# Later weights held back by a one-column copy, unit 1's scale inside unit 0's scan, stacking issued by two queues

## The chip, the cores and the metric

The kernel runs on one core of one Trainium2 chip. The metric is the device time of one execution in microseconds. A core has five engines that run beside each other, each through its own instructions in their given order: PE (TensorE, matmuls), DVE (VectorE), ACT (ScalarE), POOL (GpSimd) and SP (SyncE, which here only issues DMAs). They wait for each other through semaphores.

## What is computed

The reference runs a linear attention with a complex decay, token by token, and then a gated feed-forward layer. Batch B = 4, heads H = 8, sequence S = 768, head dimension D = 48; the layer is 384 to 1536 to 384.

```python
scale = np.minimum(mag, 0.999) / (mag + 1e-06)      # mag = |a|
a_re_n, a_im_n = (a_re * scale, a_im * scale)
for t in range(S):
    new_re = ar * S_re - ai * S_im                   # ar, ai: a at t, per head and row
    new_im = ar * S_im + ai * S_re
    S_re, S_im = (new_re + k_t v_t^T, new_im)
    y[:, :, t] = q_t @ S_re
out = ((x @ w_a) * (x @ w_b)) @ w_out                # x: y of all heads side by side
```

## The kernel before

**Units.** The sequence is cut into chunks of 128 tokens. A unit is one chunk of two of the batches, so there are NU = 12 units: units 0 to 5 are the six chunks of batches 0 and 1, units 6 to 11 those of batches 2 and 3. For each unit four things are done in turn:

1. `scale(u)` computes the factor that limits |a|, as a tile `sc` of 128 x 768: one wide square on ACT (L177), four logarithms and exponentials on ACT, and five operations on DVE (L178, L185, L188, L190, L192). In unit 0 it goes by two halves.
2. `prep(u)` multiplies a by `sc` (L210) and scans the products of the decay over the tokens: inside blocks of eight tokens (`pr` and `z`, L226 and L232, seven steps), then over the blocks through a chain of small operations `pb` and `b_t` (L261 and L267, eight pairs), then back over all tokens (L288, L293). From that it makes the scaled queries and keys in the tile `qk` (L308, L323). L277 writes the norm of the unit's decay, about the middle of `prep`. After its first lines it runs the scale of the next unit beside its own steps (the generator `sg`), but in unit 0 it does not: unit 1's scale is run at the head of `prep(1)` instead (L202 to L204). From here on, the moment when the last L308 of a unit has ended is called the moment its keys are there.
3. `stack(u)` moves `qk` by DMA into `stk`, with the real and imaginary rows of each head stacked on the partitions: ten transfers for the eight heads, two for heads 2 and 5 (L345, issued by SP).
4. `attn(u)` is the attention in 18 pieces: scores on PE (L378) times a mask on DVE (`am`, L381), transposes (L389), outputs (L418), copies of the output as a high part `xh` (L422) and the rest `xl` (L426, L429), and the running state (L437, L444).

**The feed-forward layer.** It takes fp32 operands as a high and a low part. For each unit, and for each of NF = 12 slices f of the hidden layer, `gemm1` does 18 matmuls (L481), then `h_t` and `hl` on DVE (L490, L492) and two copies on ACT (L489, L491), and `gemm2` 6 matmuls (L499), two slices later (LAG).

**The weights.** They arrive once, in 36 parts (12 slices by three matrices, 384 KB each; L124), as 64-bit words. Each part must be converted before its first use: three operations on DVE (L133, L135, L137) into one of three buffers `o_sb`, a cast of the high part on ACT (L141), a pair of matmuls on PE that leaves the low part (L146, L147), and a cast of it on ACT (L148). `split_weights` is a generator that converts one slice at each `next(ws)`.

**What sets the order.** A scheduler puts each engine's instructions into a fixed row before the kernel runs, by the order in which the code issues them, by priorities and by what it expects to be ready; the engine then takes its row strictly in order. The code issues the loads of all weights, scale 0, `prep(0)`, `stack(0)`, six slices of conversions, and then `attn(0)`, between whose pieces `prep(1)` runs on by 800 ns a piece (P1_A). Then come the slices of unit 0, with the other six conversions and the rest of `prep(1)`, 3000 ns a slice (P1_F); `stack(1)` and `attn(1)` follow inside them. The later units go the same way one unit ahead, without conversions.

The lines of issue that the change touches:

```python
    for f in range(3, NF):
        load_weights(f)
...
    drain(scale(0, a_tiles[0], z_first))
    drain(prep(0))
    stack(0)
    load_qk(1)
    p1 = prep(1)
    for _ in range(CONV_FIRST):
        next(ws)
    x_cur = new_x()
    for _ in attn(0, *x_cur):
        drain(p1, P1_A)
```

Of the kernel before, what the change touches and what calls it, by code (L numbers as in the profile page):

```python
# [8 lines left out]
F32 = mybir.dt.float32  # L9
# [13 lines left out]
NU = NBP * NCH  # L23
# [11 lines left out]
EPS = 1e-6  # L35
A2_MAX = 2.0 ** 60
ST = 8
P1_A = 800
P1_F = 3000
TOK = 2 * C  # L40
RUN = 2 * TOK + 2
NF = DF // 128
# [7 lines left out]
CONV_FIRST = 6  # L50
# [16 lines left out]
def tile_kernel(ctx: ExitStack, tc: tile.TileContext, a_d, qk_d, v_d, w_d, qn_d, kn_d, vn_d, an_d, out_d):  # L67
    nc = tc.nc
# [47 lines left out]
    raws = {}  # L116
# [1 line left out]
    def r(ap):  # L118
        return ap.bitcast(F32R)

    def load_weights(f):
        for m, (c0, n) in enumerate(WPART):
            raws[f, m] = wpool.tile([128, n, 2], U32, name=f"w{m}{f}")
            sync.dma_start(out=raws[f, m].rearrange("p c s -> p (c s)"),  # L124
                           in_=w_d[f, :, c0:c0 + n].bitcast(U32))

# [27 lines left out]
    def load_a(u):  # L154
        t = apool.tile([128, 2, W], F32, name="a_t")
        for hs in halves if u == 0 else (slice(0, W),):
            sync.dma_start(out=t[:, :, hs], in_=a_d[u, :, :, hs])
        return t

    a_tiles = {}  # L160
# [38 lines left out]
    def prep(u):  # L199
        c = u % NCH  # L200
        a_t = a_tiles.pop(u)
        if u == 1:  # L202
            yield from scale(u, a_t, a_first)
            a_tiles[u + 1] = load_a(u + 1)  # L204
        sc = sc_tiles.pop(u)
        z = zpool.tile([128, 3, W], F32, name="z") if u else z_first
        zz = z[:]
# [3 lines left out]
                              in1=sc.rearrange("p (b i e) -> p b i e", e=2, i=SUB // 2), op=ALU.mult)  # L211
        act.activation(out=z[:, 0], in_=z[:, 2], func=AF.Copy, scale=-1.0)  # L212
        yield 1700
        sg = scale(u + 1, a_tiles[u + 1], a_t) if 0 < u < NU - 1 else iter(())


        zb = z.rearrange("p s (j b e) -> p s j b e", j=SUB // 2, e=2)
# [116 lines left out]
    def load_qk(u):  # L334
        sync.dma_start(out=qk[:, :, 1, 0:2 * TOK], in_=qk_d[u])

    def stack(u):
        n = RUN if rescaled(u % NCH) else 2 * TOK
        for h in range(H):
            r0 = h * D  # L340
            while r0 < (h + 1) * D:
                j, p = divmod(r0, 128)
                m = min((h + 1) * D - r0, 128 - p)
                d0 = 2 * (r0 - h * D)
                sync.dma_start(out=stk[d0:d0 + 2 * m, h, 0:n], in_=qk[p:p + m, j, :, 0:n])  # L345
                r0 += m


# [249 lines left out]
    a_first = a_tiles[0] = load_a(0)  # L598
    load_weights(0)
    load_qk(0)  # L600
    load_weights(1)
    load_v(0)
    load_weights(2)
    a_tiles[1] = load_a(1)
    for f in range(3, NF):
        load_weights(f)

    def drain(gen, ns=None):
        if gen is None:
            return  # L610
        left = ns
        for cost in gen:
            if left is not None:
                left -= cost or 0
                if left <= 0:
                    return

    ws = split_weights()
    drain(scale(0, a_tiles[0], z_first))
    drain(prep(0))  # L620
    stack(0)
    load_qk(1)
    p1 = prep(1)
    for _ in range(CONV_FIRST):
        next(ws)
    x_cur = new_x()
    for _ in attn(0, *x_cur):
        drain(p1, P1_A)
    pend = []

    def second():
# [10 lines left out]
    for w in range(NU):  # L642
# [17 lines left out]

        for f in range(NF):
            if w == 0:
                next(ws, None)
                drain(p1, P1_F)
                if f == P1_AT:
                    drain(p1)
                    stack(1)
                    load_qk(2)
                    pgen = prep(2)
            pend.append((w, f, *gemm1(f, *x_cur), os_))  # L670
            slot()
            if len(pend) > LAG:
                second()
            slot()
            if f == STACK_AT[min(w, 4)]:
                drain(at)
                if w + 2 < NU:
                    drain(pgen)
                    stack(w + 2)
                if w + 3 < NU:  # L680
                    load_qk(w + 3)
                    pgen = prep(w + 3)
            if w > 0:
                drain(pgen, 2400)
# [70 lines left out]
```

## Time and profile before

| | |
|---|---|
| runs of the kernel | 700.78, 701.29, 702.23 us (median 701.29) |
| the profiled execution | 701.13 us, of it 699.4 from its first to its last instruction (the span) |
| granted clock of PE, mean | 0.984 |
| busy over the span | PE 656.8 us, DVE 541.8, ACT 320.2, POOL 5.6 |
| PE's first matmul of the feed-forward layer | 76.33 us |
| DMA read from and written to memory | 39.32 MB and 4.72 MB |

All times in the trace are microseconds from the start of the span. The page shows the span in 40 equal slices of 17.5 us; a digit is the busy share in tenths, and PEclk is the clock that PE was granted, in tenths of full speed:

```profile
PE   3547999999999999999999999999999999999996
DVE  6999899998889989899898989989899353232221
ACT  6357755735546255462554646356434222222221
PEclk9976999999999999999999999999999999999999
DMA  8963301513215033061431601520500500400000
```

PE is full from the fifth slice on. DVE is full from the second slice until the 29th, where the last unit's scan ends, and has little to do behind it. The weights and the first inputs come in during the first three slices. A busy PE is not PE at its peak, as matmuls overlap; what counts here is where it stands idle.

In the rows of the trace, a row that covers several instructions has a count (x2), and brackets hold an engine's idle time ahead of it and what ended that. The printed duration of a DVE operation reaches some 0.1 us into the next one, so what an operation takes from DVE is read from one start to the next.

### The profile page before, as it was taken

The numbers are of one execution on the slowest core, as the hardware profiler recorded it, in microseconds if no ns is written. First come the engines' busy times: TensorE is split into PE (matmuls) and PEld (weight loads), VectorE is DVE, ScalarE is ACT, GpSimd is POOL, SyncE is SP. The second block draws the span as 40 slices with busy tenths as digits, with TensorE's granted clock in tenths as the row PEclk, the third lists the DMA queues.
The fourth block names the chain that finished last, engine by engine and source line by source line (L and its number), as shares of the span: only waits on it lengthen the run. The fifth ranks groups of instructions, "written<-read, shape, count | busy, mean of one in ns | idle before, by whom it ended". The sixth has DMA issues, their size and how long they took to land.

```text
span 699.4 us, 14330 instructions
## 1 busy us (share of the span) xinstructions
PE 656.8 (94%) x5862; PEld 612.5 (88%) x5862; DVE 541.8 (77%) x1239; ACT 320.2 (46%) x642; POOL 5.6 (1%) x11
## 2 busy tenths in 40 slices
PE   3547999999999999999999999999999999999996
PEld 1214889899899999999999999999998999999996
DVE  6999899998889989899898989989899353232221
ACT  6357755735546255462554646356434222222221
POOL 3000000000000000000000000000000000000000
PEclk9976999999999999999999999999999999999999
DMA  8963301513215033061431601520500500400000
GB/s 316 402 258 100 112 1 46 147 44 110 87 38 182 17 120 101 16 189 46 120 100 45 168 24 46 152 82 5 163 24 13 154 24 17 106 23 2 23 1 28
DMA packets 30232, 63.94 MB, mean 91 GB/s; under 512 B 3664, under 2 KB 7248, under 8 KB 30160
## 3 DMA queue, kind: packets, MB, share of 16 engines
q1 hardware_dynamic: 26704, 58.23, 26.4%
q10 hardware_dynamic: 3456, 4.72, 1.8%
q8 instruction: 48, 0.79, 0.5%
q14 instruction: 24, 0.20, 0.1%
HBM read 39.32 MB, written 4.72 MB: 63 GB/s over the span
## 4 chain that ended last, share of the span: by engine, by line
PE 50%; DVE 38%; ACT 5%; DMA 3%; issue 2%; SPq 1%; DVEq 0%; ACTq 0%
PE ab L481 23%; PE o L499 12%; PE xp L418 4%; DVE a_t L288 4%; PE pm L378 4%; DVE qk L308 3%; DVE pr L226 3%; DVE hl L492 3%; DVE h_t L490 2%; PE pm L437 2%; DVE z L293 2%; DVE pb L261 2%; DVE z L232 2%; DMA stk<-qk 2%; PE pm L146 2%
## 5 line engine op out<-in xcount | busy, mean ns | idle before, releaser
L481 PE MATMUL ab<-xh,w 128*128 128x256 f32 x1728 | 339.3, 285 | 0.0
L481 PEld LDWEIGHTS ab<-xh,w 128*128 128x128 f32 x1728 | 276.9, 189 | 2.0 <-issue 1.4
L481 PE MATMUL ab<-xl,w 128*128 128x256 f32 x864 | 244.8, 283 | 0.0
L481 PEld LDWEIGHTS ab<-xl,w 128*128 128x128 f32 x864 | 163.0, 189 | 0.4
L499 PE MATMUL o<-w,hh 128*128 128x384 f32 x576 | 152.9, 345 | 0.0
L490 DVE TENSOR_TENSOR h_t<-ab,h_t 128x256 f32<-128x256 f32 x144 | 60.4, 419 | 80.0 <-ACT h_t L489 79.6
L489 ACT COPY h_t<-ab 128x256 f32<-128x256 f32 x144 | 53.3, 370 | 150.1 <-PE ab L481 149.1
L499 PEld LDWEIGHTS o<-w,hh 128*128 128x128 f32 x576 | 97.0, 188 | 3.5 <-issue 2.8
L491 ACT CAST hh<-h_t 128x256 fp32r<-128x256 f32 x144 | 58.0, 403 | 90.2 <-DVE h_t L490 89.6
L499 PE MATMUL o<-w,hl 128*128 128x384 f32 x288 | 97.4, 338 | 0.0
L492 DVE TENSOR_TENSOR hl<-h_t,hh 128x256 fp32r<-128x256 f32 x144 | 60.5, 420 | 20.6 <-ACT hh L491 20.5
L146 PE MATMUL ab<-o_sb,ident 128*128 128x384 f32 x42 | 28.7, 784 | 29.1 <-DVE o_sb L137 29.1
L378 PE MATMUL pm<-stk 128*128 128x128 f32 x384 | 53.6, 279 | 2.3 <-DMA stk<-qk 2.3
L499 PEld LDWEIGHTS o<-w,hl 128*128 128x128 f32 x288 | 54.1, 188 | 0.2 <-issue 0.2
L378 PEld LDWEIGHTS pm<-stk 128*128 128x128 f32 x384 | 48.7, 192 | 6.1 <-issue 3.9
L226 DVE TENSOR_TENSOR pr<-z 128x384 f32<-128x384 f32 (+1 forms) x91 | 47.2, 525 | 4.2 <-ACT z L212 2.1
L288 DVE TENSOR_TENSOR a_t<-z,b_t 128x768 f32<-128x768 f32 x48 | 44.3, 952 | 0.1
L146 PEld LDWEIGHTS ab<-o_sb,ident 128*128 128x128 f32 x42 | 9.7, 274 | 39.2 <-DVE o_sb L137 29.5
L418 PE MATMUL xp<-am,v_t 128*32 128x128 f32 x768 | 41.4, 277 | 2.3 <-DVE am L381 2.0
L308 DVE TENSOR_TENSOR qk<-qk,z 128x1536 f32<-128x1536 f32 (+1 forms) x26 | 42.4, 1629 | 0.1
L381 DVE TENSOR_TENSOR am<-pm,mask 128x512 f32<-128x512 f32 x48 | 32.8, 685 | 6.1 <-PE pm L378 6.1
L437 PE MATMUL pm<-v_t,kt 128*96 128x96 f32 x320 | 34.6, 250 | 0.1
(105 smaller groups left out, 766.4 us busy)
## 6 DMA issues: line engine op xcount, KB each, us to landing
w<-in_dram SPq DMA_DIRECT2D x36, 384.0 KB, 8.1
qk<-in_dram SPq DMA_DIRECT2D x12, 768.0 KB, 4.9
stk<-qk SPq DMA_DIRECT2D x48, 192.0 KB, 3.3
a_t<-in_dram SPq DMA_DIRECT2D x11, 768.0 KB, 4.4
v_t<-in_dram SPq DMA_DIRECT2D x24, 256.0 KB, 2.7
stk<-qk SPq DMA_DIRECT2D x24, 192.8 KB, 3.1
out_dram<-o_sb ACTq DMA_DIRECT2D x24, 192.0 KB, 1.9
stk<-qk SPq DMA_DIRECT2D x16, 128.0 KB, 3.2
```

The costliest lines, as they stand in the source:

```text
L146: pe.matmul(out=lp[:, 0:n], lhsT=ident, rhs=t, start=True, stop=False)
L226: vec.tensor_tensor(out=pr[:, :, :, o:o + n], in0=view(zz, W + at_(i) + 2 * o, [[W, 2], [-W, 2], [2, n]]), in1=tok(slice(1, 3), i - 1, o, ...
L288: vec.tensor_tensor(out=pz[:, s].rearrange("p (j b e) -> p j b e", j=SUB // 2, e=2), in0=zb[:, 1 + s], in1=view(bb, (1 + k - s) * NB, [[0, ...
L308: vec.tensor_tensor(out=qk4[:, :, k, x0:x1], in0=qk4[:, :, 1, x0:x1], in1=z[:, k].rearrange("p (j t) -> p j t", j=NJ).unsqueeze(2).broadca ...
L378: pe.matmul(out=sp[:, h4], lhsT=stk[:, h, ks], rhs=stk[:, h, qs], start=True, stop=True)
L418: pe.matmul(out=xp[qd * 32:(qd + 1) * 32, ti], lhsT=l, rhs=rr, start=st, stop=sp_, tile_position=(0, qd * 32), skip_group_check=True)
L481: pe.matmul(out=ab[:, m * TOK:(m + 1) * TOK], lhsT=r(w_ab(f, part, m * NJ + i)), rhs=r(xt[:, i, :]), start=n == 0, stop=n == 8)
L489: act.copy(out=h_t, in_=ab[:, 0:TOK])
L490: vec.tensor_tensor(out=h_t, in0=ab[:, TOK:2 * TOK], in1=h_t, op=ALU.mult)
L491: act.copy(out=r(hh), in_=h_t)
L492: vec.tensor_tensor(out=r(hl), in0=h_t, in1=hh, op=ALU.subtract)
L499: pe.matmul(out=os_[tt][:, 0:DM], lhsT=r(ht[:, ts]), rhs=r(w_t[f, 2][:, part, :]), start=(f == 0 and n == 0), stop=(f == NF - 1 and n == 2))
```

## The change

Four things are changed.

- **Weights held.** The loads of slices 0 to 2 stay at the start. Ahead of each part's load of slices 3 to 5, POOL now copies one column of unit 0's norm (written by L277 before, L276 after) into the part's buffer, and ahead of those of slices 6 to 11 one element a partition of unit 0's `qk`, where the keys' product L323 (L322 after) writes. The load overwrites the copy, so it must wait for it, and with it for that point of unit 0's scan. That makes 9 and 18 copies. SP issues the 18 behind its part of `stack(0)`.
- **Unit 1's scale** runs beside the steps of `prep(0)`; its input is loaded before the weights of slice 1, and unit 2's input right ahead of `stack(0)`'s transfers on SP.
- **Order of issue.** Three slices of conversions instead of six stand ahead of `attn(0)`, three more between its pieces, and `prep(1)` runs on only in the slices of unit 0, ahead of each slice's conversion.
- **Stacking of unit 0.** Odd heads are issued by ACT, even heads by SP. The other units' stay on SP.

```diff
+    def load_weights(f, after=None):
         for m, (c0, n) in enumerate(WPART):
             raws[f, m] = wpool.tile([128, n, 2], U32, name=f"w{m}{f}")
+            if after is not None:
+                nc.gpsimd.tensor_copy(out=raws[f, m].bitcast(F32)[:, 0, 0:1], in_=after)
             sync.dma_start(out=raws[f, m].rearrange("p c s -> p (c s)"),
...
-        if u == 1:
-            yield from scale(u, a_t, a_first)
-            a_tiles[u + 1] = load_a(u + 1)
...
-        sg = scale(u + 1, a_tiles[u + 1], a_t) if 0 < u < NU - 1 else iter(())
+        sg = scale(u + 1, a_tiles[u + 1], a_t) if u < NU - 1 else iter(())
...
-                sync.dma_start(out=stk[d0:d0 + 2 * m, h, 0:n], in_=qk[p:p + m, j, :, 0:n])
+                (act if u == 0 and h % 2 else sync).dma_start(out=stk[d0:d0 + 2 * m, h, 0:n], in_=qk[p:p + m, j, :, 0:n])
...
     load_qk(0)
+    a_tiles[1] = load_a(1)
     load_weights(1)
     load_v(0)
     load_weights(2)
-    a_tiles[1] = load_a(1)
-    for f in range(3, NF):
-        load_weights(f)
...
     drain(prep(0))
+    for f in range(3, CONV_FIRST):
+        load_weights(f, norms[:, 0, 0:1])
     stack(0)
+    for f in range(CONV_FIRST, NF):
+        load_weights(f, qk[:, 0, 1, TOK:TOK + 1])
     load_qk(1)
+    a_tiles[2] = load_a(2)
     p1 = prep(1)
-    for _ in range(CONV_FIRST):
+    for _ in range(3):
         next(ws)
     x_cur = new_x()
-    for _ in attn(0, *x_cur):
-        drain(p1, P1_A)
+    for n, _ in enumerate(attn(0, *x_cur)):
+        if n % 6 == 3:
+            next(ws)
...
             if w == 0:
+                drain(p1, P1_F)
                 next(ws, None)
-                drain(p1, P1_F)
```

How the rows of the engines move is shown at three places. Lines of the changed kernel are one or two off: L135, L137 and L139 are its conversion, L148 and L149 PE's pair, L344 the stacking, L480 the first matmuls of a slice.

On DVE, in the last steps of unit 0's scan inside the blocks, before the change (`w_138` and `w_140` are weight parts, `pr`, `z` and `tt` belong to the scan):

```order
L133 TENSOR_SCALAR o_sb<-w_138 128x384
L226 TENSOR_TENSOR pr<-z 128x4x48 x2
L232 TENSOR_TENSOR z<-pr 128x2x48 x2
L135 SCALAR_TENSOR_TENSOR o_sb<-w_138,o_sb 128x384
L226 TENSOR_TENSOR pr<-z 128x4x48 x2
L232 TENSOR_TENSOR z<-pr 128x2x48 x2
L137 SCALAR_TENSOR_TENSOR o_sb<-w_138,o_sb 128x384
L237 TENSOR_SCALAR z<-z 128x96
L133 TENSOR_SCALAR o_sb<-w_140 128x384
L244 TENSOR_TENSOR pr<-z 128x192
L135 SCALAR_TENSOR_TENSOR o_sb<-w_140,o_sb 128x384
L247 TENSOR_TENSOR tt<-pr 128x96
```

The same place after the change (`a_t` of 128x768 and `sc<-a_t,sc` are steps of unit 1's scale):

```order
L135 TENSOR_SCALAR o_sb<-w_134 128x384
L225 TENSOR_TENSOR pr<-z 128x4x48
L187 TENSOR_TENSOR a_t<-a_t 128x768
L225 TENSOR_TENSOR pr<-z 128x4x48
L231 TENSOR_TENSOR z<-pr 128x2x48 x2
L137 SCALAR_TENSOR_TENSOR o_sb<-w_134,o_sb 128x384
L190 SCALAR_TENSOR_TENSOR a_t<-a_t 128x768
L236 TENSOR_SCALAR z<-z 128x96
L192 SCALAR_TENSOR_TENSOR sc<-a_t,sc 128x768
L243 TENSOR_TENSOR pr<-z 128x192
L194 SCALAR_TENSOR_TENSOR sc<-sc,a_t 128x768
L246 TENSOR_TENSOR tt<-pr 128x96
```

Two conversion steps have gone from here and four steps of unit 1's scale have come in.

On SP, the queue around the stacking of unit 0, before the change (`w_194` to `w_198` are the last weight parts):

```order
L124 DMA w_194<-in_dram 128x768
L124 DMA w_196<-in_dram 128x768
L124 DMA w_198<-in_dram 128x768
L345 DMA stk<-qk 96x1x512 x2
L345 DMA stk<-qk 64x1x512
L345 DMA stk<-qk 32x1x512
L345 DMA stk<-qk 96x1x512 x2
L345 DMA stk<-qk 32x1x512
L345 DMA stk<-qk 64x1x512
L345 DMA stk<-qk 96x1x512 x2
L335 DMA qk<-in_dram 128x3x512
L157 DMA a_t<-in_dram 128x1536
```

After the change (`w_304` is the last part of slice 5, `w_317` the first of slice 6):

```order
L126 DMA w_301<-in_dram 128x768
L126 DMA w_304<-in_dram 128x768
L159 DMA a_t<-in_dram 128x1536
L344 DMA stk<-qk 96x1x512
L344 DMA stk<-qk 64x1x512
L344 DMA stk<-qk 32x1x512
L344 DMA stk<-qk 96x1x512 x2
L126 DMA w_317<-in_dram 128x768
L126 DMA w_320<-in_dram 128x768
```

Unit 2's `a_t` now stands ahead of the stacking, five of the ten transfers have left SP, and the 18 later parts stand behind them, with unit 1's `qk` behind those.

On PE, where unit 0's attention ends and the feed-forward layer begins, before the change (`w_336`, `w_366` and `w_396` are converted parts, `stk` is the stacked unit 0):

```order
L418 MATMUL xp<-am,v_t 32x128 x9
L389 MATMUL pm<-ident,stk 128x96
L437 MATMUL pm<-v_t,kt 96x96 x3
L426 MATMUL xp<-xh,nident 128x384
L437 MATMUL pm<-v_t,kt 96x96 x5
L481 MATMUL ab<-xh,w_336 128x256
L481 MATMUL ab<-xh,w_366 128x256
L481 MATMUL ab<-xh,w_396 128x256
L481 MATMUL ab<-xl,w_336 128x256
L481 MATMUL ab<-xh,w_336 128x256
L389 MATMUL pm<-ident,stk 128x96 x8
```

After the change (`w_658` is the low part of the third matrix of slice 5, `w_701` to `w_721` those of slice 6, `w_378` the converted first part of slice 0):

```order
L388 MATMUL pm<-ident,stk 128x96 x8
L148 MATMUL ab<-o_sb,ident 128x384
L149 MATMUL ab<-w_658,nident 128x384
L436 MATMUL pm<-v_t,kt 96x96 x8
L148 MATMUL ab<-o_sb,ident 128x384
L149 MATMUL ab<-w_701,nident 128x384
L148 MATMUL ab<-o_sb,ident 128x384
L149 MATMUL ab<-w_711,nident 128x384
L148 MATMUL ab<-o_sb,ident 128x384
L149 MATMUL ab<-w_721,nident 128x384
L480 MATMUL ab<-xh,w_378 128x256
L480 MATMUL ab<-xl,w_378 128x256
```

Pairs of the conversion now stand between the last pieces of unit 0's attention and the first matmul of the feed-forward layer; before, that matmul stood directly behind the attention. In both rows 21 parts are converted ahead of it. From the first scores of unit 3 on, the same instructions stand ahead of each later unit's scores on PE in both kernels, and only a few neighbours are swapped on PE and on DVE.

More of the change, by code (lines that the diff above doesn't have):

```diff
@@ L37 @@
 ST = 8
-P1_A = 800
 P1_F = 3000
@@ L119, in r @@
         return ap.bitcast(F32R)
-    def load_weights(f):
+    def load_weights(f, after=None):
         for m, (c0, n) in enumerate(WPART):
             raws[f, m] = wpool.tile([128, n, 2], U32, name=f"w{m}{f}")
+            if after is not None:
+                nc.gpsimd.tensor_copy(out=raws[f, m].bitcast(F32)[:, 0, 0:1], in_=after)
             sync.dma_start(out=raws[f, m].rearrange("p c s -> p (c s)"),
```

## The prediction

> **What bounds the kernel now.** I read the stages first (busy time of each engine in stretches that I cut at the places where unit 0's scan, its attention, unit 1's scan and unit 2's scan end), then the chain of waits across the last of those places.
>
> ```profile
> core 0: us, PE busy (x) PEld busy (x) DVE busy (x) ACT busy (x) POOL busy (x), PEclk, DMA share, GB/s
> 7.67:58.05 50.38, 29.50 (x54) 13.33 (x54) 49.66 (x133) 26.79 (x52) 0.00 (x0) 0.85 0.79 307
> 58.05:76.33 18.28, 14.39 (x132) 10.71 (x133) 15.96 (x29) 12.28 (x23) 0.00 (x0) 0.86 0.58 173
> 76.33:122.03 45.70, 45.67 (x308) 40.92 (x307) 45.24 (x112) 29.16 (x63) 0.00 (x0) 1.00 0.09 30
> 122.03:168.33 46.30, 46.30 (x444) 43.36 (x443) 41.78 (x93) 24.30 (x45) 0.00 (x0) 1.00 0.30 89
> ```
>
> Two things are to be seen. PE has idle time only ahead of 76.33: 20.9 us in the first row and 3.9 in the second; in the next two rows it has none. And DVE is as full: it is idle 0.7, 2.3, 0.5 and 4.5 us in the four rows, 8.0 us in all. So until 168 us two engines are full at once, and to start PE sooner is worth something only if DVE delivers sooner too.
>
> ```profile
> 166.75 1.67 DVE qk L308
> 168.44 3.36 DMA stk<-qk
> 171.93 0.46 PE pm L378 x2
> PE pm L378 <- DMA stk<-qk: 1.5, 1, 1.5
> ```
>
> These are three pieces of the chain of waits and a row of PE's waits: unit 2's keys leave DVE, are stacked by DMA, and PE, which had waited 1.5 us, starts unit 2's scores at 171.93. That is the point by which I measure the change. What comes behind it is PE's, almost without a gap. If DVE reaches unit 2's keys no sooner, PE gains nothing, whatever happens at 60 or 76 us.
>
> **The change, part by part.** First the prices on DVE, taken from start to start, since the printed durations overlap.
>
> ```profile
> 29.66 0.55 DVE L135 SCALAR_TENSOR_TENSOR o_sb<-w,o_sb 128x384 uint32<-128x384 uint32 x1
> 30.13 0.25 DVE L247 TENSOR_TENSOR tt<-pr 128x96 f32<-128x96 f32 x1
> 30.29 0.55 DVE L137 SCALAR_TENSOR_TENSOR o_sb<-w,o_sb 128x384 uint32<-128x384 uint32 x1
> 30.76 0.18 DVE L248 TENSOR_SCALAR tt<-tt 128x48 f32<-128x48 f32 x1
> 30.86 0.35 DVE L133 TENSOR_SCALAR o_sb<-w 128x384 uint32<-128x384 uint32 x1
> 31.13 0.19 DVE L261 TENSOR_TENSOR pb<-tt,b_t 128x24 f32<-128x24 f32 x1
> 31.23 0.35 DVE L133 TENSOR_SCALAR o_sb<-w 128x384 uint32<-128x384 uint32 x1
> ...
> 57.09 0.96 DVE L308 TENSOR_TENSOR qk<-qk,z 128x768 f32<-128x768 f32 x1
> ...
> 71.53 0.94 DVE L192 SCALAR_TENSOR_TENSOR sc<-sc,a_t 128x768 f32<-128x768 f32 x1
> 72.40 0.68 DVE L381 TENSOR_TENSOR am<-pm,mask 128x512 f32<-128x512 f32 x1
> 73.00 1.81 DVE L210 TENSOR_TENSOR z<-a_t,sc 128x768 f32<-128x768 f32 x2
> ```
>
> A weight part is converted by L133, L135 and L137: 0.27 + 0.47 + 0.47 = 1.21 us. An operation 768 wide is 0.87, a mask 0.60, and a small pb between other work 0.10. Unit 0's keys are complete at 57.09 + 0.96 = 58.05.
>
> *Up to unit 0's keys.* Counted in the two orders up to the last L308 of unit 0, DVE has 6 L133, 5 L135 and 5 L137 fewer now (13 parts instead of 18 and a bit): 6 x 0.27 + 10 x 0.47 = 6.3 us. It has the five steps of unit 1's scale more: 5 x 0.87 = 4.35. So most of the room is filled again by the second part of the change. The end of the chain of pb and b_t also loses its filling:
>
> ```profile
> 145.48 0.20 DVE L261 TENSOR_TENSOR pb<-tt,b_t 128x24 f32<-128x24 f32 x1
> 145.72 0.18 DVE L267 TENSOR_TENSOR b_t<-pb 128x12 f32<-128x12 f32 x1
> 145.93 0.20 DVE L261 TENSOR_TENSOR pb<-tt,b_t 128x24 f32<-128x24 f32 x1
> ...
> 77.34 0.56 DVE L226 TENSOR_TENSOR pr<-z 128x384 f32<-128x384 f32 x1
> 77.93 0.36 DVE L232 TENSOR_TENSOR z<-pr 128x192 f32<-128x192 f32 x1
> 78.33 0.57 DVE L226 TENSOR_TENSOR pr<-z 128x384 f32<-128x384 f32 x1
> ...
> 84.68 0.35 DVE L232 TENSOR_TENSOR z<-pr 128x192 f32<-128x192 f32 x1
> 84.95 0.55 DVE L137 SCALAR_TENSOR_TENSOR o_sb<-w,o_sb 128x384 uint32<-128x384 uint32 x1
> ```
>
> Where each small operation must wait for the one before it, it takes 0.22 us instead of about 0.1; eight stand so now, some 1.0 us more. Sum: -6.3 + 4.35 + 1.0, so the keys come about 1.0 us sooner, at 57.1.
>
> *From the keys to the last mask.* Before, this took until 73.00, 15.0 us. Now five parts (6.05), two z (1.74), a pr (0.47) and four masks (2.4) lie there, 10.7 us, and the waits for scores. These depend on the stacking:
>
> ```profile
> 58.08 6.78 SPq L345 DMA_DIRECT2D stk<-qk  x10
> ...
> 65.32 0.69 DVE L381 TENSOR_TENSOR am<-pm,mask 128x512 f32<-128x512 f32 x1
> ...
> stk<-qk SPq DMA_DIRECT2D x48, 192.0 KB, 3.3
> ```
>
> SP needs 0.68 us an issue. With odd heads on ACT, the last piece of the first four heads is SP's third issue instead of the fifth of one row: issue at 58.5, landing 3.3 later, scores in 0.8, first mask at 62.6 instead of 65.32. DVE gets to that mask 4.9 us behind the keys, at 62.0, so it waits 0.6; I add 0.5 for the others. The last mask ends at 68.9, **4 us sooner**. What the two issuers cost: five issues, 3.4 us, lie on ACT, and the casts L141 and L148 and unit 1's L212 stand behind them; DVE needs L212's result at about 66, so I cost this at nothing, and at up to 3 us if that cover is gone. The transfer of unit 2's a_t, now ahead of the stack on SP, is issued 2.7 us before the keys, when unit 0's last reader of that buffer is done; between nothing and 1 us for sharing the DMA engines, and I take nothing. The load of unit 1's q and k now stands behind 18 weights on SP; unit 1's L323 wants it only at 116.
>
> *From the masks to PE's big matmuls: where the 4 us stay.* PE takes its instructions in order, and the L146/L147 pairs of f = 4 to 6 now stand between attention and the first L481. PE gets to L481 when DVE has converted the 21st part. From the keys to there DVE has eight parts (9.7), two z (1.74), four masks (2.4), five steps pr and z at 0.47 + 0.27 (3.7) and one step of scale (0.87): 18.4, with the 1.1 of waits 76.6, and 1.3 for the casts and PE's pair: 77.9. Before, L481 began at 76.33, but 2.3 us of unit 0's attention came between its first matmuls:
>
> ```profile
> 77.25 0.66 PE pm L389 x8
> ...
> 78.20 1.60 PE pm L437 x16
> ...
> 90.75 2.15 PE ab L481 x18
> ```
>
> (0.7 of transposes and 1.6). On equal work that is 78.6 against 77.9, so PE is only **0.7 us** ahead.
>
> *Up to unit 2's keys.* Here the counts of all DVE lines in both orders are equal: nothing has gone, only the order is another. DVE is sooner by waits that go, less those that come:
>
> ```profile
> DVE pr L226 <- ACT z L212: 1.9, 2, 1.5
> DVE o_sb L133 <- ACT w L141: 0.6, 1, 0.6
> ```
>
> The 1.5 and the 0.6 lie between 58 and 76 and have conversions in their place now; 1.1 of new waits come. Five of unit 1's steps pr and z, which took 0.99 us unfilled, are filled now (0.74): 1.25 back, against the 1.0 lost in unit 0. In all DVE is about 1.3 us ahead on equal work, PE 0.7. Unit 2's stack lands between 0.7 and 1.3 us sooner; but PE has six L481 fewer behind it there (6 x 2.15 / 18 = 0.7 us), which it must do later. The gain is 0 to 0.6 us; I take 0.5, near the upper end, since the 1.3 of DVE rests on counted rows. From unit 3's first scores on, PE's order has the same work ahead of every unit's scores, with a few neighbours swapped on both engines, so I let the shift stay as it is. The profiled execution's own time is 701.13 us: **700.6**. The median of the runs shown is 701.29, 0.16 above that execution.
>
> **The held weights.** The 9 loads of f = 3 to 5 wait for L277 of unit 0, through a copy of one column each on POOL.
>
> ```profile
> 40.16 0.16 DVE L277 TENSOR_TENSOR chk<-n 128x6 f32<-128x6 f32 x1
> ...
> w<-in_dram SPq DMA_DIRECT2D x36, 384.0 KB, 8.1
> ...
> 0.31 0.10 POOL L743 MEMSET const-float32-0.0<- 128x1 f32 x1 [0.31 <-issue]
> ```
>
> By my count L277 ends at 40.0 now and the first conversion that needs such a weight is due at 46.1, so there are 6.1 us for POOL's copy, SP's issue and the landing. The landing is not shown for an empty queue: 8.1 us is the median in a full one, 3.3 the stack's 192 KB. I take 4, nearer to the latter because nothing else is on the queues then; the bounds are 3.3 (no stall) and 8.1 (DVE stalls 2.9). The second group is issued behind the stack at about 61 and wanted first at 68.6: covered in the same way. The copies are 27; the nearest row on POOL is 0.10 each, and beside DVE's work I take them at nothing, 2.7 if each stops DVE.
>
> **Rivals.**
> 1. *The early masks carry through* (faster). If the scheduler's places of the pairs don't hold PE, L481 begins at 72.3, and DVE's 4.5 us of waits before unit 2's keys shrink as PE's results come sooner. Against it: the order is fixed and PE's pairs stand ahead of L481. DVE's idle time bounds it: at most 8.0 us; with half of that, less the 0.7, 3.3 us: 697.8.
> 2. *The held weights come late* (slower). If the landing is the 8.1 us of the full queue, DVE, in order, stands 2.9 us at the first held weight, and unit 0's keys and all behind them come 2.9 later: 700.6 + 2.9 = 703.5. It decides from a landing of about 5 us on. Against it: the queue is empty then.
> 3. *POOL's copies stop DVE* (slower). DVE is busy 49.66 of 50.38 us where the first nine fall; if each copy takes DVE's place for its 0.10, the chain grows by 2.7: 703.3. The Trainium skill ("SBUF — State Buffer", section "SBUF: two separate sides") says that VectorE and GpSimd share a pair of ports under an exclusive lock, which a two-input VectorE operation and a GpSimd operation that reads SBUF contend for. By that rule this would happen; no row of the trace tests it, since POOL's work in it only fills memory.
> 4. *Stacking from two engines does nothing*, because ACT is held as long as SP was. The first mask would be at 64, and the last still ahead of the 21st part; by the working above the time stays within 0.5 us of the forecast, so it is inside it.
>
> **How the numbers follow.** Forecast and rival 4 together 0.46, rival 1 0.30, rival 2 0.14, rival 3 0.10. A measurement of this kernel can tell about 0.2%, 1.4 us, from no change. Faster takes rival 1 and a bit of the forecast, 0.31; same 0.45; slower rivals 2 and 3, 0.24. The forecast's own range is 699.4 to 702.4; the range of all reaches to rival 1 at 697.8 and just over rival 2, to 704.
>
> **What would show it.** Unit 0's keys at 57 (59 or later: rivals 2 or 3; a wait of DVE for a w transfer names 2, longer DVE operations beside POOL's copies name 3). Last mask of unit 0 at about 69. First L481 near 78 with PE idle before it on L146 waiting for DVE; near 72 means rival 1. Unit 1's keys near 119.5 (122.0 less the 1.3, and less 1.1 for one conversion step, an h_t and an hl that come behind them now), and PE's start on unit 2's scores at 171 or so. I am wrong if PE's idle time ahead of its first L481 falls by more than 2 us on equal work.

## The result, and the profile after

The changed kernel is slower: 706.86 us in the median of 5 runs (706.03 to 709.05) against 702.23 for the kernel before beside it, a ratio of 1.0069 with a 95% interval of 1.0054 to 1.0085. The forecast was 700.6, the range ended at 704.0. The profiled execution took 706.03 us with a span of 704.0, 4.6 more than the 699.4 before.

| us | before | forecast | after |
|---|---|---|---|
| unit 0's keys | 58.05 | 57.1 | 57.46 |
| first mask of unit 0 starts | 65.32 | 62.6 | 65.89 |
| last mask of unit 0 ends | 73.0 | 68.9 | 72.8 |
| PE's first big matmul, on equal work | 78.6 | 77.9 | 82.1 |
| unit 1's stack is issued | 122.13 | near 119.5 | 123.47 |
| PE starts unit 2's scores | 171.93 | 171 or so | 175.02 |

The stages after, cut at the ends of the same pieces of work (columns as in the first table of the prediction):

```profile
core 0: us, PE busy (x) PEld busy (x) DVE busy (x) ACT busy (x) POOL busy (x), PEclk, DMA share, GB/s
7.67:57.46 49.79, 21.55 (x38) 10.47 (x39) 48.92 (x123) 27.55 (x50) 6.31 (x9) 0.89 0.48 178
57.46:82.09 24.63, 22.73 (x173) 16.42 (x172) 20.17 (x47) 14.68 (x34) 6.87 (x18) 0.81 0.98 332
82.09:123.47 41.38, 41.10 (x265) 36.43 (x265) 40.99 (x104) 24.91 (x54) 0.00 (x0) 1.00 0.19 70
123.47:171.55 48.08, 48.08 (x455) 44.81 (x454) 42.60 (x96) 23.95 (x46) 0.00 (x0) 1.00 0.28 86
```

Add DVE's busy times: 48.92 + 20.17 + 40.99 + 42.60 = 152.68 us up to unit 2's keys, and 152.64 in the four rows of before. DVE's work is the same to 0.04 us. What differs is its idle time: 0.9 + 4.5 + 0.4 + 5.5 = 11.2 us against 8.0. By these 3.2 us unit 2's keys come later, and PE's scores behind them by 3.1. The largest part, 4.5 against 2.3, lies in the second row. The chain of waits and DVE's timeline show the place:

```profile
57.49 5.39 DMA stk<-qk
62.88 0.04 issue
62.93 0.79 PE pm L377 x2
63.72 1.28 PE ab L148 x2
65.00 0.85 PE pm L377 x4
...
171.55 3.33 DMA stk<-qk
174.88 0.14 issue
175.02 0.46 PE pm L377 x2
```

```profile
60.91 0.57 DVE L137 SCALAR_TENSOR_TENSOR o_sb<-w,o_sb 128x384 uint32<-128x384 uint32 x1
61.38 0.97 DVE L209 TENSOR_TENSOR z<-a_t,sc 128x768 f32<-128x768 f32 x1
65.89 0.69 DVE L380 TENSOR_TENSOR am<-pm,mask 128x512 f32<-128x512 f32 x1 [3.54 <-PE pm L377]
```

DVE stands 3.54 us at unit 0's first mask. A mask needs the scores of four heads. The second head, issued by ACT, lands 5.39 us after the keys, and PE waits for it. The last piece of the four is SP's third issue, of 64 KB: it starts at 58.90 and takes 5.3 us, so it lands at 64.2, 6.7 us behind the keys. Before, SP's fifth issue brought it at 64.0, 5.9 behind the keys, and the forecast had 4.7. ACT's timeline shows its five issues, and what stood behind them:

```profile
57.49 5.99 ACTq L344 DMA_DIRECT2D stk<-qk  x5
63.53 0.48 ACT L150 CAST w<-ab 128x384 fp32r<-128x384 f32 x1 [6.35 <-DMA stk<-qk]
```

The list of DMA issues of the changed kernel from 50 to 80 us, with KB each and the median us from issue to landing:

```profile
stk<-qk SPq DMA_DIRECT2D x3, 192.0 KB, 5.1
stk<-qk ACTq DMA_DIRECT2D x3, 192.0 KB, 5.4
```

And the same row of the kernel before:

```profile
stk<-qk SPq DMA_DIRECT2D x6, 192.0 KB, 3.2
```

With two issuers the ten issues end 6.0 us after the keys, where SP alone took 6.8; so 0.8 us of issuing is saved, and each transfer of 192 KB takes 2 us longer. The Trainium skill ("DMA: Bandwidth & Descriptors", section "Issuing engines are not separate DMA queues") says that DMAs issued by several engines run on the same 16 DMA engines and only the issuing time is saved. These rows agree with it: 0.8 us is what the second issuer saves. They also show a price: ACT is held by its five issues for 6 us, and the cast L150 behind them waits 6.35.

The rest of the way to the first mask is PE's. Its order has two matmuls of the conversion (L148) ahead of the scores of the third and fourth head, and its granted clock, the third number from the end, is still half there, while it was full again by 64 us before. The two rows are the changed kernel's and the one of before:

```profile
64.00:66.00 2.00, 2.00 (x8) 1.49 (x7) 0.11 (x1) 0.83 (x3) 0.39 (x4) 0.50 1.04 261
```

```profile
64.00:66.00 2.00, 1.46 (x10) 1.03 (x8) 1.58 (x4) 2.00 (x5) 0.00 (x0) 1.00 0.85 229
```

The two L148 take 1.28 us there, and another two take 0.65 from 69.67 on, where the clock is full. So the slow clock has a part in the late mask. How much of DVE's wait it makes isn't measured; no run changes the clock alone.

Of the 4.6 us, 3.1 are there at unit 2's scores. From them to the end PE is busy for 1.2 us more than before (520.0 against 518.8; six of the big matmuls, 0.7 us by the forecast's price, are among it) and idle for 0.3 us more (9.0 against 8.7). That is the other 1.5. The waits for masks that the profile lists there grow more, from 1.5 to 3.4 us, but PE's idle time as a whole doesn't.

### The profile page after: what moved, and what is told of

Its sections match the earlier page's. It is cut to its first block, busy times and chain, and to the rows that moved or that the text cites. A ratio compares the mean times of both kernels' runs of the same rounds, so it can differ in the third digit from the quotient of the medians.

```text
span 704.0 us, 14408 instructions
## 1 busy us (share of the span) xinstructions
PE 655.8 (93%) x5862; PEld 613.1 (87%) x5862; DVE 542.0 (77%) x1239; ACT 317.5 (45%) x642; POOL 18.8 (3%) x38
## 4 chain that ended last, share of the span: by engine, by line
DVE 45%; PE 41%; ACT 5%; DMA 4%; issue 2%; SPq 2%; DVEq 0%; ACTq 0%
PE ab L480 19%; PE o L498 9%; DVE qk L307 5%; DVE pr L225 4%; DVE a_t L287 4%; PE xp L417 3%; PE pm L377 3%; DVE hl L491 3%; DVE h_t L489 3%; DVE z L231 3%; DMA stk<-qk 2%; DVE pb L260 2%; DVE z L292 2%; PE pm L436 2%; DVE z L209 2%
## 5 line engine op out<-in xcount | busy, mean ns | idle before, releaser
L480 PE MATMUL ab<-xh,w 128*128 128x256 f32 x1728 | 338.7, 284 | 0.0
L480 PEld LDWEIGHTS ab<-xh,w 128*128 128x128 f32 x1728 | 276.8, 189 | 2.0 <-issue 1.6
L480 PE MATMUL ab<-xl,w 128*128 128x256 f32 x864 | 244.8, 283 | 0.0
L480 PEld LDWEIGHTS ab<-xl,w 128*128 128x128 f32 x864 | 163.0, 189 | 0.3
L489 DVE TENSOR_TENSOR h_t<-ab,h_t 128x256 f32<-128x256 f32 x144 | 60.5, 420 | 82.3 <-ACT h_t L488 82.1
L148 PE MATMUL ab<-o_sb,ident 128*128 128x384 f32 x42 | 27.5, 751 | 35.8 <-DVE o_sb L139 35.8
L148 PEld LDWEIGHTS ab<-o_sb,ident 128*128 128x128 f32 x42 | 9.9, 276 | 43.7 <-DVE o_sb L139 33.3
L307 DVE TENSOR_TENSOR qk<-qk,z 128x1536 f32<-128x1536 f32 (+1 forms) x26 | 42.4, 1631 | 0.2
```

Source lines behind the costliest of these rows:

```text
L307: vec.tensor_tensor(out=qk4[:, :, k, x0:x1], in0=qk4[:, :, 1, x0:x1], in1=z[:, k].rearrange("p (j t) -> p j t", j=NJ).unsqueeze(2).broadca ...
L480: pe.matmul(out=ab[:, m * TOK:(m + 1) * TOK], lhsT=r(w_ab(f, part, m * NJ + i)), rhs=r(xt[:, i, :]), start=n == 0, stop=n == 8)
L489: vec.tensor_tensor(out=h_t, in0=ab[:, TOK:2 * TOK], in1=h_t, op=ALU.mult)
```

## The experiments

Every time is a median beside the kernel before on the same chip (702.1 to 702.5). The theories keep their letters throughout.

**1. SP alone issues the stack; unit 2's a_t behind it; both; and two issuers alone.**

```diff
-                (act if u == 0 and h % 2 else sync).dma_start(out=stk...
+                sync.dma_start(out=stk...
```

> The changed kernel with all ten transfers of unit 0's stack issued by SP again. Theory I (two issuers cost the time: ACT is held 6 us by its five issues, 57.5 to 63.5, and each transfer takes 5.0 us to land instead of 3.1): unit 0's first mask, at 65.9 in the changed kernel, comes 7.3 us behind the keys as before, so at about 64.7 or sooner, the transfers take about 3.1 us, PE's first big matmul L480 comes at 79 to 80 instead of 82.1, and the kernel is 0 to 2 us slower than the kernel before instead of 4.6. Theory L (the 768 KB load of unit 2's a_t, issued 2.6 us ahead of the stack, fills the DMA engines): the transfers still take 4 to 5 us, and as SP issues all ten one after another the first mask comes at 66 or later; 4 to 6 us slower than before. Theory O (the new place of the conversions makes PE late, whatever the stack does): the first mask may move, L480 stays within 0.7 us of 82.1, 4 to 5 us slower than before.

Measured: 704.88 us, ratio 1.0038 (1.0026 to 1.0050), 2.5 us slower than before: about half of the loss is gone. The ten transfers take 3.1 us in the median, the first mask starts at 65.42, L480 at 81.44. No theory fits whole: the time is above theory I's 0 to 2 us, and L480 moves by only 0.65 us, as theory O says, whose time of 4 to 5 us isn't met.

```diff
+        if after is not None:
+            nc.gpsimd.tensor_copy(out=t[:, 0, 0:1], in_=after)
...
     stack(0)
+    a_tiles[2] = load_a(2, qk[:, 0, 1, TOK:TOK + 1])
...
-    a_tiles[2] = load_a(2)
```

> The changed kernel with unit 2's a_t load held, by a copy of one element a partition on POOL, until unit 0's keys are there, so that SP issues it behind the stack; still two issuers. Theory I: the transfers still take 4.5 to 5 us and ACT stays held for over 5 us; 4 to 5 us slower than the kernel before. Theory L: the transfers take about 3.3 us, ACT is held 4 us or less, the first mask comes at 63.5 to 64.5, 1 to 3 us slower than before. Theory O: L480 stays within 0.7 us of 82.1, 4 to 5 us slower than before.

Measured: 706.75, ratio 1.0076 (1.0054 to 1.0097), as slow as the changed kernel; transfers 5.1 us, ACT held 5.8. Theory L falls: the big load ahead of the stack doesn't make it land late, neither here nor in the run before, where it stood ahead of transfers of 3.1 us.

> The changed kernel with both: SP alone issues the stack, and unit 2's a_t is loaded behind it. Theories I and L together: the transfers take 3.1 us or less, the first mask comes at about 64.3, L480 at 78 to 79.5, and the kernel is within 1 us of the kernel before. Theory O: L480 within 0.7 us of 82.1, 4 to 5 us slower than before.

Measured: 702.69, ratio 1.0006 (0.9997 to 1.0014): no difference to before. So the second issuer and the place of unit 2's load together carry nearly all of the loss, 0.0063 of 0.0069. Its stages:

```profile
7.67:57.18 49.51, 22.09 (x39) 10.93 (x39) 48.74 (x122) 27.02 (x48) 6.31 (x9) 0.89 0.46 170
57.18:81.03 23.85, 21.58 (x173) 15.74 (x172) 21.57 (x48) 15.05 (x34) 8.11 (x19) 0.87 0.90 306
81.03:119.99 38.96, 38.73 (x251) 34.24 (x251) 38.71 (x97) 23.78 (x51) 0.00 (x0) 1.00 0.29 111
119.99:167.35 47.36, 47.36 (x456) 45.15 (x455) 43.68 (x98) 24.60 (x48) 0.00 (x0) 1.00 0.30 88
```

DVE is busy 152.70 us again, idle 7.0, and unit 2's stack is issued at 167.35, 1.1 sooner than before. Theory O falls by this time. But theory I's number for PE was wrong too: PE's first big matmul comes at 81.03, not near 79.

```diff
-                sync.dma_start(out=stk...
+                (act if u == 0 and h % 2 else sync).dma_start(out=stk...
```

> The kernel before with only the odd heads of unit 0's stack issued by ACT. Theory I: ACT is held 5 us or more, the transfers take 4.5 to 5 us instead of 3.1, the first mask comes 1 to 2 us later than 65.3, and the kernel is 1.5 to 3.5 us slower than before. Theory L: the transfers take about 3.3 us (no big load runs ahead of them), the first mask comes 1 to 2 us sooner, and the kernel is within 1 us of before. Theory O: within 1 us of before, whatever the mask does.

Measured: 711.98, ratio 1.0129 (1.0111 to 1.0147): 9.6 us slower than before from this one edit, far beyond every theory. Transfers 4.2 to 4.7 us for 192 KB, the first mask at 66.54 after a wait of 3.65, and unit 1's stack at 129.78 instead of 122.13. PE then stands at unit 1's scores, and its granted clock falls (first the row of PE's waits from 130 to 150 us, then windows of one microsecond, where the clock is the third number from the end):

```profile
PE pm L378 <- DMA stk<-qk: 3.7, 4, 1.9
```

```profile
135.00:136.00 1.00, 0.00 (x0) 0.00 (x0) 0.97 (x3) 0.30 (x1) 0.00 (x0) 0.96 0.84 204
136.00:137.00 1.00, 0.80 (x3) 0.58 (x3) 0.53 (x1) 0.97 (x2) 0.00 (x0) 0.50 0.93 318
...
148.00:149.00 1.00, 1.00 (x5) 0.93 (x5) 0.00 (x0) 0.48 (x1) 0.00 (x0) 0.50 0.00 0
149.00:150.00 1.00, 1.00 (x9) 0.99 (x9) 0.25 (x1) 0.08 (x1) 0.00 (x0) 0.72 0.00 0
```

From 136 to 149.6 us PE works at half clock. It is busy for 12.4 us of that, so by an estimate half of them, some 6 us, are lost, on top of the 3.7 us of waits. (149.6 is worked out from the last row's mean of 0.72.)

**2. How does the second issuer cost it?** Unit 1's scale in unit 0's part alone, then with two issuers:

```diff
-        if u == 1:
-            yield from scale(u, a_t, a_first)
-            a_tiles[u + 1] = load_a(u + 1)
...
-        sg = scale(u + 1, a_tiles[u + 1], a_t) if 0 < u < NU - 1 else iter(())
+        sg = scale(u + 1, a_tiles[u + 1], a_t) if u < NU - 1 else iter(())
...
+    a_tiles[1] = load_a(1)
     load_weights(1)
     load_v(0)
     load_weights(2)
-    a_tiles[1] = load_a(1)
...
     load_qk(1)
+    a_tiles[2] = load_a(2)
```

> The kernel before with only unit 1's scale run beside the steps of unit 0's scan (and its input loaded ahead of the weights of slice 1). In its order 17 parts instead of 18 are converted ahead of the keys, so DVE has 4.35 - 1.2 = 3.1 us more to do there and the keys come at about 61. Theory P (from the keys on PE is the bound, so its first matmul L481 on equal work, 78.6 before, sets the end): L481 on equal work at 81 to 82, 2 to 3.5 us slower than before. Theory V (the view of the prediction: DVE's sum up to unit 2's keys sets the end, and that sum is unchanged): PE starts unit 2's scores at 172 plus or minus 0.5, and the kernel is within 1 us of before.

Measured: 705.09, ratio 1.0046 (1.0031 to 1.0060), 2.9 us slower, as theory P says, while unit 2's stack is issued sooner than in any other run:

```profile
164.80 6.63 SPq L342 DMA_DIRECT2D stk<-qk  x10
```

That is 3.6 us ahead of before. One of PE's big matmuls starts at 79.67, the next only at 81.30, so on equal work PE begins at 81.2, 2.6 us later than before. So DVE's arrival at unit 2's keys alone doesn't set the end.

> The same with the odd heads of unit 0's stack issued by ACT. Theory H (the price of the second issuer is what waits on ACT behind its held issues; with two issuers alone that was unit 1's scale, whose square waited 4.6 us, and unit 1's keys came 7.6 us later): the scale is done here, only casts wait, and the step from the run before this one to this one is 1 to 4 us instead of the 9.6 measured without the scale's move. Theory D (the price is the longer landing of the transfers, whatever waits on ACT): the step is about as large as there, 8 to 10 us.

Measured: 706.77, ratio 1.0066 (1.0051 to 1.0080), a step of 1.7 us, in theory H's bounds and far from D's, though the transfers take 5.0 us and ACT is held 6.03.

```diff
     stack(0)
+    with tc.high_priority(offset=4000):
+        for _ in range(2):
+            act.copy(out=a_first...,
+                     in_=qk[:, :, 0, 0:512]...)
```

> The changed kernel with SP alone issuing the stack and unit 2's a_t behind it (as in the run of both, 702.7), and two added conversions on ACT from unit 0's keys on, of 3072 elements a partition each, some 6 us together by the 1.50 us of a square of 1536: ACT is held as by its five issues, the transfers are not. Theory H: the casts behind come 5 to 6 us late, PE's pairs wait for them, and the kernel is 2 to 4 us slower than the run of both. Theory D: the transfers land in 3.1 us, the first mask stays near 65.4, within 1 us of the run of both.

Measured: 702.87, ratio 1.0015 (1.0003 to 1.0027), like the run of both. The two operations, 2.75 us each, held ACT from 56.13 to 61.86 with one cast between them, and theory H's 2 to 4 us didn't come. The run is weaker than meant: it began 1.3 us ahead of the keys, let that cast through, and has another order on PE than the run of both.

```diff
-                sync.dma_start(out=stk...
+                (nc.gpsimd if u == 0 and h % 2 else sync).dma_start(out=stk...
```

> The kernel before with the odd heads of unit 0's stack issued by POOL, which has nothing else to do there, instead of by ACT (711.98 measured with ACT, 9.6 us slower than before). Theory H (what waits on ACT behind its held issues, above all unit 1's scale, is the price): unit 1's square L179 isn't held, unit 1's keys come within 1.5 us of 122.1 instead of 129.8, and the kernel is 0 to 3 us slower than before. Theory D (two issuers make the transfers land later, and PE and DVE pay): 7 to 10 us slower than before, as with ACT.

Measured: 705.06, ratio 1.0035 (1.0022 to 1.0048), 2.6 slower, theory H's time, though not its picture: unit 1's stack is issued at 129.10, as late as with ACT, though nothing is held on ACT here. So ACT's hold isn't needed to make unit 1's keys late. The transfers land later still, and DVE stands at masks for 6.5 us:

```profile
stk<-qk SPq DMA_DIRECT2D x3, 192.0 KB, 6.5
stk<-qk POOLq DMA_DIRECT2D x3, 192.0 KB, 5.2
```

Here PE has other work in its order in front of unit 1's scores, waits 0.4 for that stack, and keeps its full clock. So PE's standing at unit 1's scores and the slow clock behind it are what the run with ACT has more; by the estimates above they are large enough for the 7 us between the two. Whether ACT's hold is what put PE there isn't shown.

**3. The order.** In all five kernels so far with ACT or POOL issuing the odd heads, the program's order on DVE has unit 0's first mask 10 to 12 instructions behind the keys, with SP alone 14 to 16. In the kernel before, the change of the issuer alone moves it from 15 to 10. That the scheduler, which fixes the order when the kernel is built, reckons with a sooner stack is an inference; the runs show only where it puts the mask.

```diff
-            with tc.high_priority(offset=ATTN_FIRST):
+            with tc.high_priority(offset=-140 if u == 0 and i == 0 and hg == 0 else ATTN_FIRST):
                 vec.tensor_tensor(out=am, in0=sp, ...
```

> The changed kernel as it is (two issuers, unit 2's a_t ahead of the stack), with only the priority of unit 0's first mask lowered by 140, so that in DVE's order it stands 18 instructions behind the keys instead of 11 (16 in the kernels with SP alone). Theory S (the scheduler reckons that two issuers bring the stack sooner and puts the mask earlier in DVE's order; the transfers don't land sooner, so DVE stands at it): DVE's wait of 3.5 us at the first mask falls below 1 us, and the kernel is 2 to 3.5 us faster than the changed one, 703.4 to 704.9. Theory D or H (longer landing, or ACT held, cost PE the time): within 1 us of the changed kernel's 706.9, whatever DVE's wait does.

Measured: 704.48, ratio 1.0029 (1.0016 to 1.0041), as theory S has it: with both issuers and transfers of 5.2 us, 0.0040 of 0.0069 are back. PE's clock stays at half until 67 us here too, so these 0.0040 aren't the clock's.

```profile
65.06 0.36 DVE L135 TENSOR_SCALAR o_sb<-w 128x384 uint32<-128x384 uint32 x1 [1.81 <-ACT w L143]
...
67.86 0.68 DVE L380 TENSOR_TENSOR am<-pm,mask 128x512 f32<-128x512 f32 x1
```

The first mask is no longer waited for; a wait of 1.81 for a cast held on ACT stands in its place, which is the part of theory H that this order shows.

```diff
-                (act if u == 0 and h % 2 else sync)
+                (act if u == 0 and h > 5 else sync)
```

> The changed kernel with only heads 6 and 7 of unit 0's stack issued by ACT, two issues; unit 2's a_t stays ahead of the stack. In its order the first mask stands 16 instructions behind the keys, as with SP alone. Theory S: DVE waits under 1 us at the first mask, ACT is held under 2 us, and the kernel is like the run with SP alone (704.9) or better, 703 to 705. If two issuers cost by themselves, however few issues: 706 or more.

Measured: 705.05, ratio 1.0043 (1.0031 to 1.0055), just above theory S's bound, like SP alone. DVE waits 1.24 at the first mask, ACT is held 2.1 us.

**4. The other parts of the change**, each against the run of both (1.0006):

```diff
+    for f in range(3, NF):
+        load_weights(f)
...
-        load_weights(f, norms[:, 0, 0:1])
...
-        load_weights(f, qk[:, 0, 1, TOK:TOK + 1])
```

> The run of both (702.7) without POOL's holds: all weights are loaded from the start, as before. In its order 17 parts instead of 13 are converted ahead of the keys, so the keys come at 57.2 + 4 x 1.21 = 62.0. Theory P: PE has 4 pairs of 0.82 us fewer to do behind the keys, 3.3 us against 4.8 of later keys: L481 on equal work about 1.5 us later, 0.5 to 2.5 us slower than the run of both. Theory W (the held loads cost time themselves, by the copies on POOL or by transfers beside the stack): 1 us or more faster than the run of both. Theory V: within 1 us of it.

Measured: 705.20, ratio 1.0041 (1.0026 to 1.0057). Without the holds it is 2.5 us slower; theory W falls. The keys come at 60.00, as four parts more stand ahead of them, but PE reaches unit 2's scores only 0.4 us later than in the run of both (171.14 against 170.78). Most of the 2.5 us come behind that, and the runs don't show why.

```diff
-    load_weights(2)
...
-    for f in range(3, CONV_FIRST):
+    for f in range(2, CONV_FIRST):
```

> The run of both with slice 2's weights held as well, by the same copies: in its order 10 parts instead of 13 are converted ahead of the keys. Theory P: the keys come 3 x 1.21 = 3.6 us sooner, at about 53.6, and PE has three pairs more behind them, 2.5 us: 0 to 1.5 us faster than the run of both, so 701.2 to 702.7. Theory V (DVE's sum up to unit 2's keys is unchanged): within 0.5 us of it. If the held loads come late: DVE waits for a transfer of w, and it is slower by that wait.

Measured: 702.49, ratio 1.0008 (0.9999 to 1.0018). The keys come at 54.7, but unit 2's stack at 170.31 instead of 167.35: what was put off comes back.

The third part of the change (order of issue) is undone with these lines of before:

```diff
-    for _ in range(3):
+    for _ in range(CONV_FIRST):
         next(ws)
...
-        if n % 6 == 3:
-            next(ws)
+        drain(p1, 800)
...
-                drain(p1, P1_F)
                 next(ws, None)
+                drain(p1, P1_F)
```

> The run of both (702.7) with the order of issue of before (six slices of conversions ahead of unit 0's attention, unit 1's scan drained between its pieces, and each slice's conversion ahead of its part of the scan). In its order 15 parts instead of 13 are converted ahead of the keys and 19 instead of 21 ahead of PE's first matmul of the feed-forward layer. Theory P/V together (the later of two bounds decides: PE's first matmul on equal work plus 620.6, DVE's keys of unit 2 plus 531): the keys come 2.4 us later, at 59.6, PE's matmul on equal work between 81 and 83: 701 to 704.5. If the order of issue is what helps or harms by itself: more than 2 us away from 702.7.

Measured: 706.27, ratio 1.0062 (1.0046 to 1.0077): 3.9 us slower than the run of both by the ratios, and outside the 701 to 704.5. The premise about the keys didn't hold: the trace has 13 parts converted ahead of them, as in the run of both, and they come at 57.30. The 19 ahead of PE's first big matmul are there. So the new order of issue helps by itself, and the two bounds don't explain by how much.

The pairs left out, on the run of both. The low parts of these slices are then not computed, so the output isn't the reference's:

```diff
+                if f in (5, 6):
+                    act.copy(out=r(lo), in_=t)
+                    continue
                 pe.matmul(out=lp[:, 0:n], lhsT=ident, rhs=t, start=True, stop=False)
```

> The run of both (SP alone, unit 2's a_t behind the stack, 702.7) with PE's pairs L148 and L149 of slices 5 and 6 left out (the low parts are cast from the converted weights instead), six pairs that lie behind the keys. DVE's work is the same. Theory P (from the keys on PE's work sets the end, 0.82 us a pair): 3.5 to 5 us faster than the run of both, 697.7 to 699.2. Theory V (DVE's sum sets it): within 1 us of the run of both.

Measured: 701.57, ratio 0.9987 (0.9978 to 0.9997), only 1.1 us faster than the run of both (1.3 by the ratios); theory P falls as the whole story.

```profile
75.86 0.48 PE L485 MATMUL ab<-xh,w 128*128 128x256 f32 x2
```

PE starts its big matmuls 5.2 us sooner than in the run of both, but unit 2's stack now leaves at 169.22, 1.9 later. So PE's gain doesn't reach the end: DVE, which comes later now, is as near a bound as PE.

The other six pairs are left out by `f in (1, 2)` in the same place.

> The same with the pairs of slices 1 and 2 left out, six pairs that lie ahead of the keys, where PE waits for DVE most of the time. Theory P: within 0.7 us of the run of both, since they fill PE's idle time. If it is PE's whole work that counts, wherever it lies: 3.5 to 5 us faster as well.

Measured: 702.61, ratio 1.0009 (1.0000 to 1.0018): against the run of both nothing is gained, so PE's work ahead of the keys is free, as theory P says.

No version tried beats the kernel before with the computation whole.

## Why the prediction was wrong, point by point

- **The step that failed is the stacking**, "issue at 58.5, landing 3.3 later, scores in 0.8, first mask at 62.6". It took issuing to be the limit and the landing time of one issuer for that of two. Forecast were 5.5 us from the keys to the first mask; it takes 8.4 (7.3 before). Of the 2.9 us that are missing, 2.0 are the landing of the first four heads (6.7 us behind the keys instead of 4.7), and 0.9 are PE, which does the mask's last scores behind two L148 and at half clock. In the other runs it takes 8.0 to 9.5 us with the odd heads on a second issuer (10.0 where the mask is put later in the order), and 6.6 to 8.5 with SP alone. DVE got to the mask 4.9 us behind the keys, just as forecast; its wait there, put at 0.6, is 3.54.
- **Rival 4 was dismissed wrongly.** It said that two issuers do nothing, and that the time then stays within 0.5 us. The first half was near the truth. The second overlooked that the order already had the mask early, so that a stack which isn't sooner leaves DVE standing. That is shown by the lowered priority, 2.8 us back with the same transfers.
- **ACT's hold, "at nothing, and at up to 3 us if that cover is gone"**: five issues were 6.0 us, not 3.4. Its share in the loss lies inside those 3 us where it could be seen (1.81 us of DVE's wait), but isn't separated from the order. With POOL as second issuer DVE stands even longer at the masks (6.5 us), with no hold on ACT.
- **Unit 2's a_t ahead of the stack, "I take nothing"**: with two issuers no difference is to be seen (1.0076 with it moved, 1.0069 with it in place). With SP alone, moving it gives 1.0038 to 1.0006, 2.2 us. The transfers take 3.1 us in both runs and the keys of unit 2 differ by 0.3 us; why the rest differs stays open.
- **Keys at 57.1**: 57.46. The sum -6.3 + 4.35 + 1.0 was right to 0.4 us; its terms weren't measured one by one.
- **DVE's work up to unit 2's keys unchanged, 1.3 us less idle**: the first is exact (152.64, 152.68, 152.70). The second came true, as 1.0, where the stacking is SP's and the load is behind. In the changed kernel it is 3.2 more idle instead.
- **First L481 at 77.9**: 82.1, and 81.0 even in the run of both. This is a second step that failed: with the stacking mended, DVE is 1.1 us sooner at unit 2's keys and the time is still no better. I counted when DVE has the 21st part converted. PE's own list was left out: 13 pairs instead of 18 stand ahead of the first scores, so five pairs of about 0.82 us (0.65 for L148 and 0.17 for L149 in the chain), 4.1 us, moved from PE's idle time to where it is full: in the changed kernel PE has no idle time from 62.9 to 82.1.
- **Unit 2's scores as the measuring point**: too simple. One run reaches that stack 3.6 us sooner and is 2.9 slower, another has PE 5.2 sooner and wins 1.1. The later of PE and DVE comes nearer to what decides, but two runs (without the holds, and with the old order of issue) are slower than that alone explains.
- **Rival 1** (masks carry through) did not come, since the last mask ended only 0.2 us sooner. **Rival 2**: no wait of DVE for a held weight; the first is converted at 46.36. What the text ahead of the prediction says of the second group needs a correction: the last L307 rewrites that element of `qk`, so its copies are released at 57.5, with the keys, and its loads begin at 63.97. **Rival 3**: POOL's copies did not stop DVE; below.

## What to carry to other kernels

Where an order is fixed ahead, an edit can move the consumers forward in it; if the data isn't there sooner, they stand there, in order, with all that is behind them. So check in the order where the waiting instruction went, and price the case "not sooner" with that place. A second issuer saved 0.8 us of issuing here, made each transfer longer by more, and held its engine for as long as its issues took. When two engines are full at once, sum both lists up to the same point.

## What the runs showed of the hardware

- **POOL's copies are slow beside a full DVE.** A POOL copy of one element a partition took 0.70 us on average in the group of nine, and one took 5.15 us in the run of both, which ended when DVE fell idle at 62.4; the 18 behind it took 3.02 together. (In the changed kernel the first of the 18 took 4.87 and also ended when DVE fell idle.)

```profile
39.92 6.31 POOL L125 COPY w<-chk 128x1 f32<-128x1 f32 x9 [33.57 <-DVE chk L278]
57.30 5.15 POOL L159 COPY a_t<-qk 128x1 f32<-128x1 f32 x1 [11.07 <-ACT w L143]
62.39 3.02 POOL L125 COPY w<-qk 128x1 f32<-128x1 f32 x18
```

DVE hardly noticed: the second step of a conversion, L137, took 0.57 us in the changed kernel beside such copies, 0.55 in the run of both beside the one of 5.15, and 0.56 (as L135) before without any. So it is POOL that waits here, not DVE, as rival 3 had it. That a lock makes it wait isn't shown by these rows.
- **After PE stood, its clock stayed at half for 13.6 us** (136 to 149.6 in the run with two issuers alone), though PE was busy for 12.4 of them; it had small gaps at 137 and at 144, and none from 139 to 144.
- **A second issuer lengthens each transfer**: 192 KB in 3.2 us with one issuer, 4.2 to 4.7 with ACT beside SP and nothing large ahead of them, 5.1 and 5.4 in the changed kernel, 5.2 to 6.5 with POOL.
